# A third attention half turned by the matrix engine ahead of the first MoE unit, and weights of groups two and three brought in one tile a unit

## The chip, the cores and the metric

The kernel runs on one core of a Trainium2 chip. The metric is the device time of one execution in microseconds. Of the engines, TensorE (PE) does the matmuls, VectorE (DVE), ScalarE (ACT) and GpSimd (POOL) the element-wise work, and SyncE (SP) issues nearly all DMA transfers.

## The reference

Three layers follow each other: a linear attention with a gate, a feed-forward layer (called MoE in the code) with a rational activation, and a second one with a softmax-like activation and a layer norm.

```python
# attention: B=4, H=8, S=768, D=48
for t in range(S):
    state = alpha[:, :, t, :, None] * state + np.einsum('bhd,bhe->bhde', k[:, :, t], v[:, :, t])
    y[:, :, t] = np.einsum('bhd,bhde->bhe', q[:, :, t], state)
# layer 1: 3072 tokens x 384 -> 2048 -> 384
h = x @ w_in
P = a[0] + a[1] * h + a[2] * h**2 + a[3] * h**3
Q = 1.0 + np.abs(b[0]) * np.abs(h) + np.abs(b[1]) * h**2
x = (P / (Q + 1e-06)) @ w_out
# layer 2: 384 -> 1024 -> 384
h = x @ w_in2
solu = h * softmax(h)
y = (layernorm(solu) * g_ln) @ w_out2
```

Both layers' weights are 64-bit floats in memory; the attention's inputs are 32-bit.

## The kernel before, in words

**Chunks and halves.** The 768 positions are cut in six chunks of 128 positions by 4 batches, 512 tokens each. A chunk's attention is done in two halves (two batches each), so there are twelve halves, numbered from 0. For a half, keys and queries are needed transposed (head dimension on partitions) and multiplied by running products of the gate alpha. Halves below NPE (two of them, 0 and 1) are turned by TensorE: `a_turn` makes, for each of two parts, three turns (alpha, key, query) of eight matmuls against the identity into a PSUM tile `tp`, on which VectorE runs its scans (`Pp`, `Rp`) and a product; `a_back` turns the keys back on TensorE (`kp`). The other halves are turned by VectorE in `a_dve`: stream transposes, two long scans, a product, two back-transposes, and then a round trip through DRAM (`a_move_qk`, `a_move`) that brings the pieces to their places. The turned query and key then go through `a_pe` on TensorE: scores `sc`, outputs `y`, the state update `u`, and `Sbd`, the state. The result of a half is the layer's input `xt`, in a high and a low part.

**Units.** Layer 1 is cut into 96 units, 16 a chunk, of 128 hidden features. `m_up(u)` does nine 512-column matmuls into `hp`, which lies in one of three PSUM banks with the tag "h". ScalarE makes Abs, two Squares, Ln and Exp of it. VectorE closes the activation with four operations, the last being `fin[u]`; in the "mixed" units (even ones below 24) VectorE has three and GpSimd two. Then `gh` (ScalarE) and `gl` (GpSimd) are the high and the low part, and `m_down` of the unit, nine more matmuls, comes four units later (LAG). A bank of `hp` is free for the unit three later when `fin` is done.

**Weights.** A weight tile comes as 64-bit words (`st` or `words`). `split_w` folds them to 32-bit floats in three VectorE operations (a shift, and two that fold), ScalarE copies the high part and GpSimd subtracts it to leave the low part. Layer 1's weights are in four groups, one for four units of a chunk, of seven tiles each: three of w_in (128x512), four of w_out (128x384). Groups 0 and 1 are folded ahead of unit 0; groups 2 and 3 (`w1_slots`) while units 0 to 7 of chunk 0 run, two tiles a unit. The place in which the folds work on is set by `stage["bank"]`: with "at" or "x2" the middle value `fp` is in PSUM, and with an empty string it is `ft` in SBUF.

**Order.** The instructions' order on each engine is the one in which the code makes them, changed by a planner that hoists an instruction where its inputs allow; `later`, `pin` and `issue_after` keep an instruction behind a given one (`fin` of some units before, for example). In each turn of the main loop the code makes a step of the next half's attention, a weight tile, an up-product and a down-product. HOLD sets from which unit a half's preparation may start, PRE how many weight tiles are folded at four places of the prologue, G1 by how many units the folds stay behind. The coefficients of the activation (the tile `co`) are worked out from a and b in 22 operations on VectorE and ScalarE.

Of the kernel before, what the change touches and what calls it, by code (L numbers as in the profile page):

```python
# [7 lines left out]
F32 = mybir.dt.float32  # L8
# [22 lines left out]
def kernel(  # L31
# [31 lines left out]
    NPE = 2  # L63
    HOLD = {2: (4, 2), 3: (13, 2)}
# [46 lines left out]
    def consts():  # L111
# [16 lines left out]
        nc.vector.tensor_scalar(cf, cf, C_MIN, None, ALU.max)
        nc.vector.reciprocal(rc, cf)
        nc.vector.scalar_tensor_tensor(beta, lin, 0.5, rc, ALU.mult, ALU.mult)  # L130
        nc.vector.tensor_tensor(t, beta, beta, ALU.mult)
        nc.vector.tensor_tensor(t, t, cf, ALU.mult)
        nc.vector.tensor_scalar(bad[:, 4 * NCH + 2:], t, BETA * BETA, None, ALU.is_gt)
        nc.vector.tensor_scalar(beta, beta, B_MAX, -B_MAX, ALU.min, ALU.max)
        nc.vector.tensor_tensor(t, beta, beta, ALU.mult)
        nc.vector.tensor_tensor(base, base, rc, ALU.mult)
        nc.vector.tensor_tensor(rest, base, t, ALU.subtract)
        nc.vector.tensor_tensor(a0s, a0s, rc[:, 1:2], ALU.mult)
        nc.vector.tensor_tensor(back, cf[:, 1:2], rc[:, 0:1], ALU.mult)
        nc.vector.tensor_tensor(back, back, sign, ALU.mult)  # L140
# [972 lines left out]
```

## Time and profile before

| what | value |
|---|---|
| median of three runs | 781.0 us (779.27, 781.0, 783.73) |
| the profiled execution | 778.71 us |
| its span, from the first to the last instruction | 776.7 us |
| granted clock of TensorE, mean | 0.970 |
| TensorE matmul busy | 731.5 us, 94% |
| VectorE busy | 628.9 us, 81% |
| ScalarE busy | 540.3 us, 70% |
| GpSimd busy | 362.5 us, 47% |

The difference of 2.0 us between the profiled execution and its span is what lies around the first and the last instruction. Shares are means over a prologue (attention halves 0 to 2 and two weight groups), the long loop of units, and layer 2, so the bound is read by stretch. Granted clock is in parts of the full 2.4 GHz.

### The profile page before, as it was taken

Reading aid. Unit: us, or ns where it says so; the run is one execution under the profiler, and the core shown is the slowest. Engines: PE = TensorE matmul, PEld = TensorE weight load, DVE = VectorE, ACT = ScalarE, POOL = GpSimd, SP = SyncE. Lnnn points to the kernel's source line nnn. Section 1 sums busy time; section 2 is a strip of 40 time slices with the busy share of each in tenths; the row PEclk is TensorE's granted clock in tenths of the full one; section 3 lists DMA queues with packets and bytes.
Section 4 is the critical chain, followed back from the end, with each engine's and each line's share of the span. In section 5 each row is a group of like instructions: output and inputs, shape, how many; then the busy total and the mean of one; then the engine's idle time right before and its main releaser. Section 6 shows DMA issues by size and latency. Waiting matters only on the chain.

```text
span 776.7 us, 13952 instructions
## 1 busy us (share of the span) xinstructions
PE 731.5 (94%) x4988; PEld 608.4 (78%) x4988; DVE 628.9 (81%) x1097; ACT 540.3 (70%) x998; POOL 362.5 (47%) x314
## 2 busy tenths in 40 slices
PE   4865989999999999999999999999999999999996
PEld 4754777878887787778877788888888989988996
DVE  5997999979998989989898876478887698877630
ACT  3446867867977888788878887788965555555541
POOL 4464878666654355434544433342243343452322
PEclk9957999999999999999999999999999999999999
DMA  7999324275737382717544340730025353541653
GB/s 177 289 295 279 61 81 111 89 224 169 186 121 166 114 207 88 184 47 219 124 144 102 124 82 1 281 127 1 1 82 120 101 131 91 129 111 49 140 118 78
DMA packets 87279, 101.75 MB, mean 131 GB/s; under 512 B 34464, under 2 KB 63136, under 8 KB 87200
## 3 DMA queue, kind: packets, MB, share of 16 engines
q1 hardware_dynamic: 87104, 100.67, 48.0%
q8 instruction: 41, 0.67, 0.4%
q14 instruction: 38, 0.31, 0.1%
q10 hardware_dynamic: 96, 0.10, 0.0%
HBM read 60.59 MB, written 27.56 MB: 113 GB/s over the span
## 4 chain that ended last, share of the span: by engine, by line
DVE 18%; PE 18%; ACT 6%; DMA 3%; SPq 3%; issue 2%; POOL 1%; ACTq 0%; DVEq 0%; POOLq 0%
PE x2p L693 6%; PE hp L648 6%; DVE room L807 3%; SPq L817 3%; DVE room L790 2%; ACT jk L792 2%; PE op L831 2%; DVE sm L786 2%; DVE room L805 2%; PE h L767 2%; DMA L<-room 1%; DVE sm L802 1%; DVE sm L803 1%; DVE p L674 1%; DVE sm L804 1%
## 5 line engine op out<-in xcount | busy, mean ns | idle before, releaser
L682 POOL TENSOR_TENSOR gl<-p,gh 128x512 fp32r<-128x512 f32 x96 | 128.4, 1338 | 198.7 <-ACT gh L681 110.6
L648 PE MATMUL hp<-xt,g 128*128 128x512 f32 x432 | 115.3, 410 | 8.4 <-DVE p L672 7.8
L648 PE MATMUL hp<-xt,w 128*128 128x512 f32 x432 | 110.0, 397 | 4.4 <-DVE p L679 4.4
L648 PEld LDWEIGHTS hp<-xt,g 128*128 128x128 f32 x432 | 82.9, 196 | 29.3 <-DVE p L672 8.0
L831 PE MATMUL op<-w2oh,ln 128*128 128x384 f32 x384 | 101.9, 339 | 0.6 <-DVE ln L823 0.6
L693 PE MATMUL x2p<-gh,g 128*128 128x512 f32 x288 | 100.2, 399 | 2.3 <-ACT x2e L701 2.3
L823 POOL TENSOR_TENSOR ln<-L,ln 128x1024 fp32r<-128x1024 f32 x22 | 54.5, 2482 | 100.8 <-ACT ln L822 96.4
L648 PEld LDWEIGHTS hp<-xt,w 128*128 128x128 f32 x432 | 81.1, 190 | 23.6 <-DVE p L679 5.7
L677 DVE SCALAR_TENSOR_TENSOR w<-w,co,hp 128x512 f32<-128x512 f32 x84 | 62.0, 738 | 44.8 <-ACT hp L676 44.1
L693 PE MATMUL x2p<-gh,w 128*128 128x512 f32 x288 | 96.5, 392 | 0.0
L767 PE MATMUL h<-w2ih,x 128*128 128x512 f32 x288 | 90.8, 394 | 0.0
L655 ACT ACTIVATE p<-hp,co 128x512 f32<-128x512 f32 x96 | 65.8, 685 | 11.1 <-POOL gl L682 10.8
L676 ACT ACTIVATE hp<-ah 128x512 f32<-128x512 f32 x84 | 50.1, 596 | 32.9 <-DVE p L674 32.0
L831 PEld LDWEIGHTS op<-w2oh,ln 128*128 128x128 f32 x384 | 70.1, 188 | 2.2 <-DVE ln L823 1.0
L674 DVE SCALAR_TENSOR_TENSOR p<-p,co,hp 128x512 f32<-128x512 f32 x84 | 61.8, 736 | 9.7 <-ACT p L655 9.1
L656 ACT ACTIVATE w<-ah,co 128x512 f32<-128x512 f32 x96 | 69.3, 723 | 0.4
L693 PEld LDWEIGHTS x2p<-gh,g 128*128 128x128 f32 x288 | 54.6, 191 | 17.5 <-ACT x2e L701 5.0
L653 ACT ACTIVATE ah<-hp 128x512 f32<-128x512 f32 x96 | 56.6, 589 | 14.5 <-PE hp L648 11.5
L681 ACT ACTIVATE gh<-p 128x512 fp32r<-128x512 f32 x96 | 59.9, 624 | 7.9 <-DVE p L679 5.1
L831 PE MATMUL op<-w2ol,ln 128*128 128x384 f32 x192 | 65.0, 339 | 0.0
L693 PEld LDWEIGHTS x2p<-gh,w 128*128 128x128 f32 x288 | 54.1, 188 | 11.7
L767 PEld LDWEIGHTS h<-w2ih,x 128*128 128x128 f32 x288 | 53.9, 188 | 11.7
(183 smaller groups left out, 1569.7 us busy)
## 6 DMA issues: line engine op xcount, KB each, us to landing
L<-room SPq DMA_DIRECT2D x96, 128.0 KB, 2.3
qk_d<-qk SPq DMA_DIRECT2D x10, 771.0 KB, 4.1
st<-in_moe_w_out_dram SPq DMA_DIRECT2D x18, 384.0 KB, 5.0
st<-in_moe_w_in_dram SPq DMA_DIRECT2D x12, 512.0 KB, 4.9
qks<-qk_d SPq DMA_DIRECT2D x20, 257.0 KB, 5.0
ra<-in_alpha_dram SPq DMA_DIRECT2D x48, 96.0 KB, 2.3
rk<-in_k_dram SPq DMA_DIRECT2D x48, 96.0 KB, 2.7
rq<-in_q_dram SPq DMA_DIRECT2D x48, 96.0 KB, 2.4
```

The source lines that it names most:

```text
L648: last["PE", u] = nc.tensor.matmul(hp, lhsT=wi[n](w, kt, o), rhs=xts[c][:, kt, xx, :], start=(kt == 0 and w == 0 and xx == 0), stop=(kt == ...
L653: nc.scalar.activation(ah, hp, AF.Abs)
L655: nc.scalar.activation(p, hp, AF.Square, bias=co[:, 7:8])
L656: nc.scalar.activation(w, ah, AF.Square, bias=co[:, 6:7])
L674: nc.vector.scalar_tensor_tensor(p, p, a1, hp, ALU.add, ALU.mult)
L677: nc.vector.scalar_tensor_tensor(w, w, rest, hp, ALU.add, ALU.mult)
L681: last["ACT", u] = nc.scalar.activation(gh, p, AF.Copy)
L682: last["POOL", u] = nc.gpsimd.tensor_tensor(gl, p, gh[:].bitcast(F32), ALU.subtract)
L693: nc.tensor.matmul(x2ps[c][d], lhsT=wo[n](w, o, d), rhs=gg, start=(f == 0 and w == 0 and gg is gh), stop=(f == NF1 - 1 and w == 1),)
L767: nc.tensor.matmul(hp[:, 512 * n:512 * n + 512], lhsT=x2s[c][:, kt, x, CH * b:CH * b + CH], rhs=w2[w][:, kt, 512 * n:512 * n + 512], start ...
L823: (nc.vector if s in FASTS else nc.gpsimd).tensor_tensor(lo, L, hi.bitcast(F32), ALU.subtract)
L831: nc.tensor.matmul(op, lhsT=x[:, 128 * f:128 * f + 128], rhs=w2[w][:, f, :], start=(f == 0 and x is hi and w == "oh"), stop=(f == NF2 - 1 ...
```

## The change

Six things are changed together. NPE is 3, so that half 2 is turned by TensorE, ahead of unit 0 and into the banks "h", and its round trip through DRAM goes. The coefficients are worked out on GpSimd (but for one reciprocal) after half 0's turn. The words of groups 2 and 3 are asked for at units 0 and 3, and folded one tile a unit in units 1 to 15 except 11, no longer two a unit in 0 to 7. Group 2's folds work in PSUM ("at"), as do those of before; group 3's in SBUF, as before. The preparation of half 4, beside half 3's attention, starts with unit 14 instead of 13, and one weight tile fewer is folded at the second place of the prologue. Units 0 and 2 are not mixed any more.

```diff
-    NPE = 2
-    HOLD = {2: (4, 2), 3: (13, 2)}
+    NPE = 3
+    HOLD = {2:(4,2),3:(14,2)}
...
-    PRE = (1, 1, 0, 0)
+    PRE = (1, 0, 0, 0)
...
-    G1 = 99
+    G1 = 2
+    PACE = {u: 1 for u in range(1, 16) if u != 11}
...
-    MIX = lambda u: u < 24 and u % 2 == 0
+    MIX = lambda u: 3 < u < 24 and u % 2 == 0
...
-        nc.vector.tensor_tensor(back, cf[:, 1:2], rc[:, 0:1], ALU.mult)
+        nc.gpsimd.tensor_tensor(back, cf[:, 1:2], rc[:, 0:1], ALU.mult)
...
-                t = (ps_hp if i < 2 else ps_ap).tile([128, B, CH], F32, name="tp", tag="h" if i < 2 else "at")
+                t = (ps_hp if i < NPE else ps_ap).tile([128, B, CH], F32, name="tp", tag="h" if i < NPE else "at")
...
+        words2 = {}
+
+        def w1_fetch(n):
...
+            words2[n] = (order, t, raw)
+
+        def w1_slots(n):
+            if n not in words2:
+                w1_fetch(n)
+            order, t, raw = words2[n]
+            stage["bank"] = "at" if n == 2 and fast else ""
...
-            _run(a_turn(0), a_pe(0), a_turn(1), a_pe(1), pre)
+            _run(a_turn(0), a_pe(0))
+            coefficients()
+            _run(a_turn(1), a_pe(1), pre)
             clear()
             pre = w1_group(1)
             take(pre, NA)
-            _run(a_load(2, ("ra", "rk")))
-            with tc.issue_after(marks[0, 1].ins):
-                _run(a_prep(2))
-            _run(a_move_qk(2))
+            _run(a_load(2))
...
-                    if f % 4 == 0:
-                        _run(prep)
-                        if f:
-                            stage["bank"] = ""
-                        prep = w1_slots(f // 4 + 2) if f < 8 else iter(())
-                    with later(G1):
-                        take(prep, 1)
+                    if f == 0:
+                        w1_fetch(2)
+                        prep = chain(w1_slots(2), w1_slots(3))
+                    if f == 3:
+                        w1_fetch(3)
...
-                    with later(G1):
-                        take(prep, 1)
+                    with later(G1 if u < NF1 - 4 else 1):
+                        take(prep, PACE.get(u, 0))
```

The line numbers of the kernel after are 8 to 17 higher than before (the turn of `a_turn` is L355 before and L363 after; `split_w`'s three folds are L540, L543, L544 before and L548, L551, L552 after; `fin` is L672 in a mixed and L679 in another unit before, L689 and L696 after).

**TensorE ahead of unit 0.** In the order before, behind the last turn of half 1 (`tp<-ident,rq`) come the matmuls that take the high part off half 0's result (`minus`), half 0's and 1's keys turned back, the scores and outputs of half 1, and then the first up-product (`hp`).

```order
L355 MATMUL tp<-ident,rq 64x128 x6
L466 MATMUL y<-xt,minus 128x256 x3
L385 MATMUL kp<-ident,qks 128x96 x8
L483 MATMUL u<-vns,kns 64x48 x16
L413 MATMUL sc<-qk_403 128x128 x8
L413 MATMUL sc<-qk_404 128x128 x8
L437 MATMUL y<-A,vn_202 32x128 x32
L466 MATMUL y<-xt,minus 128x256 x2
L648 MATMUL hp<-xt,g_136 128x512 x3
L466 MATMUL y<-xt,minus 128x256
```

In the order after, in the same place:

```order
L474 MATMUL y<-xt,minus 128x256 x3
L363 MATMUL tp<-ident,ra 64x128 x8
L393 MATMUL kp<-ident,qks 128x96 x8
L363 MATMUL tp<-ident,rk 64x128 x8
L491 MATMUL u<-vns,kns 64x48
L363 MATMUL tp<-ident,rq 64x128 x8
L491 MATMUL u<-vns,kns 64x48 x15
L421 MATMUL sc<-qk_398 128x128 x4
L363 MATMUL tp<-ident,ra 64x128 x8
L421 MATMUL sc<-qk_398 128x128 x4
L421 MATMUL sc<-qk_399 128x128 x4
L363 MATMUL tp<-ident,rk 64x128 x8
L421 MATMUL sc<-qk_399 128x128 x4
```

Behind it the keys, the turns of half 2 (`ra`, `rk`, `rq`, twice, 48 matmuls in all) now stand among the scores of half 1. The up-product, which had its first three matmuls among the attention's last, comes behind them.

**VectorE at unit 0.** In the order before, from unit 0's first operation (`hp<-p,co,hp`, L666) and unit 1's (L674) to unit 0's last (L672); `words` are group 2's tiles, `Sbd` is half 1's state:

```order
L666 SCALAR_TENSOR_TENSOR hp<-p,co,hp 128x512
L674 SCALAR_TENSOR_TENSOR p<-p,co,hp 128x512
L496 TENSOR_TENSOR Sbd<-u,end 48x8x48 x2
L540 TENSOR_SCALAR fp<-words 128x512 x2
L543 SCALAR_TENSOR_TENSOR fp<-words,fp 128x512
L671 SCALAR_TENSOR_TENSOR hp<-hp,co,ah 128x512
L543 SCALAR_TENSOR_TENSOR fp<-words,fp 128x512
L677 SCALAR_TENSOR_TENSOR w<-w,co,hp 128x512
L544 SCALAR_TENSOR_TENSOR ft<-words,fp 128x512
L672 SCALAR_TENSOR_TENSOR p<-w,hp 128x512
```

After, up to unit 0's last operation (the first L696) and unit 1's (the second):

```order
L691 SCALAR_TENSOR_TENSOR p<-p,co,hp 128x512 x2
L504 TENSOR_TENSOR Sbd<-u,end 48x8x48 x2
L694 SCALAR_TENSOR_TENSOR w<-w,co,hp 128x512 x2
L695 SCALAR_TENSOR_TENSOR hp<-w,hp 128x512 x2
L691 SCALAR_TENSOR_TENSOR p<-p,co,hp 128x512
L548 TENSOR_SCALAR fp<-words 128x512
L696 SCALAR_TENSOR_TENSOR p<-p,co,hp 128x512
L548 TENSOR_SCALAR fp<-words 128x512
L696 SCALAR_TENSOR_TENSOR p<-p,co,hp 128x512
```

Ahead of unit 0's last operation there were five operations on words, now there is one; the unit has four of its own instead of three.

**VectorE at group 3's first tiles.** In the order after, from the last operation of unit 11 (L696) to unit 12's first (L683); `ft<-words` with no `fp` are the folds in SBUF:

```order
L696 SCALAR_TENSOR_TENSOR p<-p,co,hp 128x512
L548 TENSOR_SCALAR ft<-words 128x512
L552 SCALAR_TENSOR_TENSOR ft<-words,ft 128x512
L551 SCALAR_TENSOR_TENSOR ft<-words,ft 128x512
L552 SCALAR_TENSOR_TENSOR ft<-words,ft 128x512
L548 TENSOR_SCALAR ft<-words 128x512
L551 SCALAR_TENSOR_TENSOR ft<-words,ft 128x512
L552 SCALAR_TENSOR_TENSOR ft<-words,ft 128x512
L548 TENSOR_SCALAR ft<-words 128x384
L551 SCALAR_TENSOR_TENSOR ft<-words,ft 128x384
L552 SCALAR_TENSOR_TENSOR ft<-words,ft 128x384
L683 SCALAR_TENSOR_TENSOR hp<-p,co,hp 128x512
```

Before, where the first tile of group 3 is folded, between units 4 (its last operation is just ahead) and 6; `alT` and `qk` are half 3's chain:

```order
L540 TENSOR_SCALAR ft<-words 128x512
L666 SCALAR_TENSOR_TENSOR hp<-p,co,hp 128x512
L678 SCALAR_TENSOR_TENSOR hp<-w,hp 128x512
L309 SCALAR_TENSOR_TENSOR alT<-alT,d_112 128x774
L543 SCALAR_TENSOR_TENSOR ft<-words,ft 128x512
L679 SCALAR_TENSOR_TENSOR p<-p,co,hp 128x512
L671 SCALAR_TENSOR_TENSOR hp<-hp,co,ah 128x512
L312 TENSOR_TENSOR qk<-qk,alT 128x2x3x128
L540 TENSOR_SCALAR ft<-words 128x512
L544 SCALAR_TENSOR_TENSOR ft<-words,ft 128x512
L674 SCALAR_TENSOR_TENSOR p<-p,co,hp 128x512
L672 SCALAR_TENSOR_TENSOR p<-w,hp 128x512
```

Before, the seven tiles stand between the last operation of unit 4 and that of unit 11, one or two operations at a time between the units' own. After, the first four stand nearly without a break between the last operations of unit 11 and the first of unit 12, the other three behind that.

## Rows read from the trace of the kernel before

**Rows 1.** Windows: us, busy us (count) by engine, PEclk, DMA share, GB/s
```profile
40.00:60.00 20.00, 15.33 (x107) 12.99 (x108) 19.92 (x34) 8.98 (x19) 12.19 (x10) 0.51 1.00 279
60.00:80.00 20.00, 12.16 (x72) 9.71 (x71) 15.44 (x28) 13.59 (x25) 11.28 (x11) 0.76 0.97 270
80.00:100.00 20.00, 20.00 (x96) 16.09 (x96) 20.00 (x39) 17.72 (x37) 16.75 (x18) 0.97 0.24 65
```

**Rows 2.** TensorE's timeline: start, us, instructions, in brackets the wait ahead
```profile
75.25 4.21 PE L648 MATMUL hp<-xt,g 128*128 128x512 f32 x9 [7.84 <-DVE p L672]
...
109.12 2.23 PE L648 MATMUL hp<-xt,w 128*128 128x512 f32 x9
...
118.42 3.85 PE L648 MATMUL hp<-xt,w 128*128 128x512 f32 x9 [3.98 <-DVE p L679]
```

**Rows 3.** ScalarE's timeline, end of chunk 0
```profile
170.22 0.69 ACT L701 ACTIVATE x2e<-x2p,co 128x512 f32<-128x512 f32 x1 [1.25 <-DMA w2i_d<-st]
```

**Rows 4.** Groups by line and shape, VectorE, 0 to 65.5 us: half 2's chain
```profile
L300 DVE TENSOR_TENSOR_SCAN P<-alT,d 128x774 f32<-128x774 f32 x1 | 2.5, 2544 | 0.0
L309 DVE TENSOR_TENSOR_SCAN alT<-alT,d 128x774 f32<-128x774 f32 x1 | 2.0, 1980 | 0.0
L316 DVE STREAM_TRANSPOSE alT<-qk 128x384 f32<-128x384 f32 x2 | 1.6, 851 | 0.0
L282 DVE STREAM_TRANSPOSE alT<-ra 128x256 f32<-128x256 f32 x2 | 1.2, 598 | 0.0
L312 DVE TENSOR_TENSOR qk<-qk,alT 128x768 f32<-128x768 f32 x1 | 0.9, 944 | 0.0
L287 DVE STREAM_TRANSPOSE alT<-ra 128x128 f32<-128x128 f32 x2 | 0.8, 384 | 0.0
```

**Rows 5.** The same view: scans and products of halves 0 and 1
```profile
L370 DVE TENSOR_TENSOR_SCAN Rp<-tp,Rp,d 128x127 f32<-128x127 f32 x16 | 6.6, 458 | 0.0
L366 DVE TENSOR_TENSOR_SCAN Pp<-tp,d 128x128 f32<-128x128 f32 x16 | 5.4, 403 | 5.0 <-PE tp L355 5.0
L374 DVE TENSOR_TENSOR qks<-tp,Rp 128x512 f32<-128x512 f32 x2 | 1.4, 685 | 0.1
```

**Rows 6.** The same view: coefficients, the longest and the shortest
```profile
L137 DVE TENSOR_TENSOR co<-co 128x2 f32<-128x2 f32 x1 | 0.7, 726 | 0.0
L121 DVE TENSOR_SCALAR co<-ab 128x1 f32<-128x1 f32 x1 | 0.1, 125 | 0.0
```

**Rows 7.** Groups by line and shape, GpSimd, 0 to 65.5 us
```profile
L427 POOL COPY end<-qks 128x8 f32<-128x8 f32 x1 | 0.2, 190 | 0.0
```

**Rows 8.** SyncE's timeline, the last words of group 1
```profile
49.26 0.37 SPq L533 DMA_DIRECT2D st<-in_moe_w_out_dram  x1
```

**Rows 9.** The page's DMA issues: count, KB each, us to landing
```profile
st<-in_moe_w_out_dram SPq DMA_DIRECT2D x18, 384.0 KB, 5.0
```

**Rows 10.** VectorE's timeline, the last fold of group 1
```profile
62.51 0.55 DVE L544 SCALAR_TENSOR_TENSOR ft<-st,fp 128x384 int32<-128x384 int32 x1 [0.22 <-POOL g L560]
```

**Rows 11.** TensorE's timeline: turns, and keys turned back
```profile
11.11 1.07 PE L355 MATMUL tp<-ident,rk 128*64 128x128 f32 x16
19.15 1.98 PE L355 MATMUL tp<-ident,ra 128*64 128x128 f32 x16 [5.00 <-DMA ra<-in_alpha_dram]
33.39 2.02 PE L385 MATMUL kp<-ident,qks 128*128 128x96 f32 x16 [0.64 <-ACT xt L469]
```

**Rows 12.** The page's costliest groups: an operation of an unmixed unit
```profile
L674 DVE SCALAR_TENSOR_TENSOR p<-p,co,hp 128x512 f32<-128x512 f32 x84 | 61.8, 736 | 9.7 <-ACT p L655 9.1
```

**Rows 13.** Groups by line and shape, VectorE, 60 to 165 us: folds
```profile
L544 DVE SCALAR_TENSOR_TENSOR ft<-words,ft 128x512 int32<-128x512 int32 x3 | 5.3, 1772 | 0.0
L543 DVE SCALAR_TENSOR_TENSOR ft<-words,ft 128x512 int32<-128x512 int32 x3 | 2.7, 897 | 0.0
L540 DVE TENSOR_SCALAR ft<-words 128x512 int32<-128x512 int32 x3 | 2.2, 728 | 0.0
L544 DVE SCALAR_TENSOR_TENSOR ft<-words,fp 128x512 int32<-128x512 int32 x3 | 2.0, 678 | 0.0
```

More of the change, by code (lines that the diff above doesn't have):

```diff
@@ L130, in consts @@
[L130 to L137, printed above, removed]
@@ L138, in consts, with coefficients @@
-        nc.vector.tensor_tensor(a0s, a0s, rc[:, 1:2], ALU.mult)
-        nc.vector.tensor_tensor(back, cf[:, 1:2], rc[:, 0:1], ALU.mult)
-        nc.vector.tensor_tensor(back, back, sign, ALU.mult)
+    def coefficients():
+        sb = const.tile([128, 2], F32, name="sb")
+        nc.gpsimd.tensor_scalar(sb, bb, 0.0, 2.0, ALU.is_ge, ALU.mult)
+        nc.gpsimd.tensor_scalar(sb, sb, 1.0, None, ALU.subtract)
+        nc.gpsimd.tensor_tensor(babs, bb, sb, ALU.mult)
+        cf, lin, rc, beta, rest, t, base = (co[:, 2 * x:2 * x + 2] for x in range(7))
+        nc.gpsimd.tensor_copy(cf[:, 0:1], babs[:, 1:2])
+        nc.gpsimd.tensor_copy(lin[:, 0:1], babs[:, 0:1])
+        nc.gpsimd.tensor_scalar(sign, ab[:, 3:4], 0.0, 2.0, ALU.is_ge, ALU.mult)
+        nc.gpsimd.tensor_scalar(sign, sign, 1.0, None, ALU.subtract)
+        nc.gpsimd.tensor_tensor(cf[:, 1:2], ab[:, 3:4], sign, ALU.mult)
+        nc.gpsimd.tensor_tensor(lin[:, 1:2], ab[:, 2:3], sign, ALU.mult)
+        nc.gpsimd.tensor_tensor(base[:, 1:2], ab[:, 1:2], sign, ALU.mult)
+        nc.gpsimd.tensor_tensor(a0s, ab[:, 0:1], sign, ALU.mult)
+        nc.gpsimd.memset(base[:, 0:1], QC)
+        nc.gpsimd.tensor_scalar(bad[:, 4 * NCH:4 * NCH + 2], cf, C_MIN, None, ALU.is_lt)
+        nc.gpsimd.tensor_scalar(cf, cf, C_MIN, None, ALU.max)
+        nc.vector.reciprocal(rc, cf)
+        nc.gpsimd.tensor_scalar(beta, lin, 0.5, None, ALU.mult)
+        nc.gpsimd.tensor_tensor(beta, beta, rc, ALU.mult)
+        nc.gpsimd.tensor_tensor(t, beta, beta, ALU.mult)
+        nc.gpsimd.tensor_tensor(t, t, cf, ALU.mult)
+        nc.gpsimd.tensor_scalar(bad[:, 4 * NCH + 2:], t, BETA * BETA, None, ALU.is_gt)
+        nc.gpsimd.tensor_scalar(beta, beta, B_MAX, -B_MAX, ALU.min, ALU.max)
+        nc.gpsimd.tensor_tensor(t, beta, beta, ALU.mult)
+        nc.gpsimd.tensor_tensor(base, base, rc, ALU.mult)
+        nc.gpsimd.tensor_tensor(rest, base, t, ALU.subtract)
+        nc.gpsimd.tensor_tensor(a0s, a0s, rc[:, 1:2], ALU.mult)
+        nc.gpsimd.tensor_tensor(back, cf[:, 1:2], rc[:, 0:1], ALU.mult)
+        nc.gpsimd.tensor_tensor(back, back, sign, ALU.mult)
@@ L249, in a_load @@
                     t = slot(3, 2 + x, nm)[:, :16 * D + 16]
-                elif i == 0 and nm == "rq":
+                elif i in (0, 2) and nm == "rq":
                     t = slot(3, 5, nm)[:, :16 * D + 16]
@@ L463, in a_pe @@
                 nc.scalar.activation(hi, y2[z], AF.Copy)
-                if i < NPE + 2:
+                if i < 4:
                     for a in range(n):
@@ L899, in pin @@
             if n <= now[0] < NU and fast:
-                for e, u in (("PE", now[0]), ("ACT", now[0] - n), ("POOL", now[0] - n)):
+                for e, u in (("PE", now[0] if ("PE", now[0]) in last else now[0] - 1), ("ACT", now[0] - n), ("POOL", now[0] - n)):
                     stack.enter_context(tc.issue_after(last[e, u].ins))
@@ L944, in network @@
                 if fast and u < NF1:
[L945 to L951 removed]
+                    if f == 0:
[3 more added lines that the diff above has]
+                        w1_fetch(3)
+                if fast and u == NF1:
+                    _run(prep)
                 m_up(u)
                 if fast and u < NF1:
[L954 to L955 removed]
+                    with later(G1 if u < NF1 - 4 else 1):
+                        take(prep, PACE.get(u, 0))
             if u == NU:
```

13 lines of the change are left out of this document (removed).

## The prediction, written before the changed kernel was run

> **What bounds the kernel now.** I read first the table of busy times by stretch. From 80 us on TensorE is busy all the time, 20.00 of 20 us [rows 1], and what is saved ahead of that point reaches the end of the program, one for one, as long as no new gap opens behind it. Ahead of it VectorE is the full engine: 19.92 of 20 us at 40 to 60, with the DMA engines full as well (share 1.00), while TensorE has 4.7 us free at a granted clock of 0.51. At 80 to 100 VectorE is full again (20.00) beside TensorE: there each unit's VectorE work, the words of weight groups two and three and half 3's chain share one queue. At 60 to 80 VectorE has 4.6 us free, since it waits for ScalarE and for words.
>
> Second I read TensorE's timeline for the gaps in the loop [rows 2]. One is 7.84 us long, up to 75.25: the fourth up-product wants the bank of unit 0, whose last VectorE operation ends at about 75.2. The other is 3.98 us, up to 118.42, for the same kind of reason seven units later. Each is followed by nine matmuls at the lower level, 1.2 GHz: 3.85 us after the second gap, where the same nine take 2.23 us at 109.12. So the gap at 118 costs 3.98 + 1.62 = 5.6 us. Chunk 0's result is first read at 170.22, after a wait of 1.25 us put down to a DMA [rows 3]; behind that I expect no difference.
>
> **The change part by part.** The profiled execution took 778.71 us, of which 776.7 are the span; the median of the three runs is 781.0, 2.3 above it. The sum is made against 778.71, and 2.3 is added at the end.
>
> *Half 2 turned by TensorE, and the coefficients: the prologue.* VectorE loses half 2's chain ahead of unit 0 [rows 4]: scans 2.54 and 1.98, two back-transposes 1.6, three pairs of transposes like the 1.2 one (3.6) and three like the 0.8 one (2.4), and the product 0.94; together 13.0. It gains what one turned half costs [rows 5]: half of 6.6 and 5.4 for the scans (6.0), 1.4 for its two products, and some 0.6 for end values and reciprocals: 8.0. Of the coefficients nineteen operations leave: three long ones, the longest 0.73 and the others estimated at 0.55 each, and sixteen short ones, for which I take 0.14 from the shortest shown, 0.125 [rows 6]; that is 1.8 + 2.2 = 4.0. Net on VectorE: −13.0 + 8.0 − 4.0 = −9.0. In the order of the instructions the same shows: unit 0's first VectorE operations now stand where the last words of group 1 end, with no half-2 transpose between.
>
> GpSimd gets some 27 operations of the coefficients. The nearest row is a copy of 128x8 elements at 0.19 us [rows 7], so 5.1 us, spread over a stretch where it is busy 12.19 of 20 [rows 1]. That work is covered; uncovered it would be the whole 5.1, since unit 0's squares need them.
>
> What VectorE gives up is not all gained, since the words must land. The last words of group 1 are issued at 49.26 and such a transfer lands 5.0 us later [rows 8, 9]; three operations on a 128x384 tile, the last one 0.55 us [rows 10], make 1.65, so 55.9 against 63.06 now (62.51 + 0.55): −7.1 is all that the transfers allow. The queue past which loads move is SP's: half 2's third load comes ahead of the last words, one tile of words fewer does; I set these against each other. TensorE has 48 turning matmuls more ahead of unit 0: sixteen took 1.07 us at 11.11 and 1.98 at 19.15 [rows 11], so 3.2 to 5.9 us, and it has 4.7 free. At the slower price 1.2 would stick out, and the turns share the three banks with the first up-products, so that these can no longer begin among the attention matmuls as three of them do before. I take −6.5, between −4 (turns at the low clock, one bank late by an operation of VectorE) and −9 (the transfers land sooner, since the DMA share falls when half 2's two round trips through memory go).
>
> *Half 2's keys and values in the loop.* Eight more pairs of matmuls that turn half 2's keys back stand in the full stretch: sixteen instructions at 2.02 [rows 11]. TensorE is full there, so +2.0; below, 0, if they fall into one of the gaps of [rows 2].
>
> *Units 0 and 2 not mixed, and the pace.* Each of the two units has one VectorE operation more, 0.736 [rows 12], so +1.5. Unit 0 however now has one word operation ahead of its last, where it had five. Four fewer at 0.68 [rows 13] make −2.7 for the gap at 75. The words come back between units 1 and 8 where VectorE is full, so this holds only as far as TensorE has something to do meanwhile: between −1.2 and +1.5; I take −0.5.
>
> *The gap at 118.* Group 2 comes one tile a unit, so units 4 to 7 carry less and this gap can vanish: −5.6. But the seven tiles of group 3, which stood among units 5 to 11, now begin at unit 11, four of them in a row between the last operation of unit 11 and the first of unit 12, and three more, with half 4's chain, between units 12 and 15. They are in SBUF throughout, and their three operations take 0.73 + 0.90 + 1.77 = 3.4 us a 128x512 tile [rows 13]. So the gap can move there. I take 0 for the two together; the ends are −5.6 and +9.
>
> Sum: −6.5 + 2.0 − 0.5 + 0 = −5.0, so 773.7 for an execution like the profiled one, and 776.0 against the median.
>
> The fold of 1.77 us in SBUF is 2.6 times the same fold with its input in PSUM (0.68) [rows 13]. By the Trainium skill (SBUF — State Buffer, Who interferes with whom) a VectorE instruction with two SBUF inputs contends with a GpSimd instruction that reads SBUF, and the pair of ports is locked for the whole instruction; the trace agrees with its 1.77 to 0.68. By that rule the coefficients on GpSimd would speak against this change too: if each of their 5.1 us held up a two-input operation of VectorE, the prologue would gain 5.1 less, and the sum would be +0.1.
>
> **Rivals.**
> A: the gap at 118 vanishes and nothing takes its place. For it: units 4 to 7 carry one tile each instead of two, and VectorE's work up to unit 15 falls. Against: VectorE stays full from 80 to 140. −5.0 − 5.6 = −10.6, so 770.4.
> B: the gain is eaten by VectorE. Units 12 to 15 each carry a tile of 3.4 beside four operations of 0.736 (2.9), 6.3 a unit, where TensorE needs 4.1 (two times nine matmuls: 4.5 by the nine in 2.23 of [rows 2], 3.75 by the 96 in 20.00 of [rows 1], and I take the middle). Four units fall 2.2 each behind, 8.8; the four units by which down-products lag behind up-products give back about half, 4.1 of it. +4.7 on the forecast: 780.7. For it: the full VectorE of [rows 1]. A second way to the same end: GpSimd's 5.1 us of coefficients hold up VectorE's folds for as long, as the slow fold of [rows 13] beside a busy GpSimd lets one fear; −5.0 + 5.1 gives 781.1. I give it 0.06 of B's chance. The rule of the Trainium skill cited above is that mechanism.
> C: slower. Unit 12's up-product needs the third tile of group 3. Three tiles are 10.2 us of VectorE around the last operation of unit 11; TensorE has cleared the down-products of units 8 to 10 by then and has only unit 11's, half of 4.1, to do. It stands for 8.1 us and comes back at the low clock, 1.6 more: +9.7, 785.7. It decides if the third tile is in place more than about 3.5 us after TensorE has come to that product, which would cost more than the gap at 118 did. Against: if VectorE lags by less than now, the tiles begin sooner.
> That half 2 is not ready for TensorE ahead of unit 0 (its loads late) would take the −6.5 away and leave 782.5; I see it as a part of B.
>
> **How the numbers follow.** Forecast (772 to 779) 0.40, A 0.20, B with what is like it 0.22, C 0.18. The range leaves out the far half of C and the far ends of A: 767.5 to 785.0; for the forecast alone 772 to 779. About 0.5% (3.9 us) is what a measurement of this kernel can tell from no change: faster, below 777.1, is A and most of the forecast, less what B's neighbours take: 0.55. Slower, above 784.9, is most of C: 0.15. Same: 0.30.
>
> **What would show it.** Right, if VectorE's last word operation of group 1 ends near 56.5, the gap ahead of the fourth up-product ends some 7 us sooner, and chunk 0's first read is near 165. The part on the keys is right if sixteen such matmuls stand in the loop at 2 us. A shows as no wait above 1 us on TensorE between 80 and 165; C as one long wait of unit 12's up-product for group 3's third tile, with nine matmuls near 3.9 behind it; B as several short waits for VectorE between units 12 and 16. Wrong altogether, if TensorE's first up-product begins no sooner than now since the turns wait at 0.5 of the clock.

## The result: 0.57% slower, and the profile after

The changed kernel takes 784.96 us (median of 20 runs, 781.32 to 792.07) against 782.16 (20 runs, 777.65 to 786.93): a ratio of 1.0057, interval 1.0035 to 1.0080 (the ratio goes by all the runs; the two medians alone give 1.0036). I had forecast 776.0, a ratio of 0.994. The sign is wrong.

The profiled execution of the kernel after took 787.51 us, with a span of 785.8 and a mean clock of 0.974. It lies 2.5 above its median, as that of before lies under its own, so the two profiles are 9.1 us of span apart where the medians are 2.8 apart. A second profile of each (below) gives 5.8 us. What the two pairs share is the reading. Of the 20 executions 14 lie between 781.3 and 786.4 and six between 787.5 and 792.1, and both profiles (787.51 and 790.82) are like the six, so the waits read below may be longer than those of an execution near the median.

First the windows of the kernel after, columns as in [rows 1]; the last one runs from ScalarE's first operation of unit 3 to that of unit 32.

```profile
40.00:60.00 20.00, 17.65 (x215) 15.19 (x212) 16.83 (x36) 9.04 (x19) 11.53 (x13) 0.86 1.08 293
100.00:120.00 20.00, 19.09 (x190) 16.22 (x183) 13.60 (x21) 17.09 (x33) 13.52 (x13) 1.00 0.15 52
140.00:160.00 20.00, 12.98 (x177) 9.96 (x176) 15.92 (x29) 16.54 (x33) 12.06 (x12) 0.87 0.22 41
160.00:180.00 20.00, 15.90 (x63) 11.85 (x62) 19.37 (x33) 12.74 (x24) 14.64 (x13) 0.96 0.42 136
77.70:253.50 175.80, 160.88 (x1245) 126.88 (x1244) 155.50 (x251) 131.15 (x244) 110.03 (x103) 0.98 0.48 124
```

The same stretch of the kernel before, unit 3 to unit 32:

```profile
79.50:245.80 166.30, 160.62 (x1238) 129.49 (x1238) 157.23 (x248) 129.85 (x240) 114.99 (x105) 0.97 0.51 137
```

So unit 3 is 1.8 us sooner, and the stretch to unit 32 is 9.5 longer (175.8 against 166.3). TensorE's busy time is the same (160.9 and 160.6); its idle time is 14.9 instead of 5.7. Behind unit 32 the two differ by 1.4 (532.3 and 530.9). −1.8 + 9.5 + 1.4 = 9.1, the difference of the spans.

VectorE, full at 40 to 60 in [rows 1], now idles 3.2 us there, and 6.4 at 100 to 120. The gap of [rows 2] at 118 is gone. TensorE's idle time lies at 140 to 190 instead, as its timeline shows (start, us, instructions, the wait ahead):

```profile
73.44 2.07 PE L665 MATMUL hp<-xt,g 128*128 128x512 f32 x4 [6.49 <-DVE p L696]
...
158.51 3.77 PE L665 MATMUL hp<-xt,g 128*128 128x512 f32 x9 [6.04 <-DVE p L696]
...
169.98 2.35 PE L665 MATMUL hp<-xt,g 128*128 128x512 f32 x9 [1.58 <-DVE p L696]
...
176.80 2.33 PE L665 MATMUL hp<-xt,g 128*128 128x512 f32 x9 [2.20 <-DVE alT L302]
...
186.32 2.33 PE L665 MATMUL hp<-xt,g 128*128 128x512 f32 x9 [2.67 <-DVE p L689]
```

The first of these rows is the fourth up-product; the other four are the up-products of units 16, 18, 19 and 21. Their waits make 12.5 us, and the nine matmuls at 158.51 pay 1.4 more at the low clock (3.77 against 2.33). The wait at 158 is for unit 13's last VectorE operation. VectorE's timeline shows why that one is late:

```profile
139.02 1.56 DVE L552 SCALAR_TENSOR_TENSOR ft<-words,ft 128x384 int32<-128x384 int32 x1
142.54 0.76 DVE L683 SCALAR_TENSOR_TENSOR hp<-p,co,hp 128x512 f32<-128x512 f32 x1 [1.97 <-ACT p L672]
144.57 0.76 DVE L688 SCALAR_TENSOR_TENSOR hp<-hp,co,ah 128x512 f32<-128x512 f32 x1 [1.27 <-ACT ah L685]
...
148.01 0.68 DVE L691 SCALAR_TENSOR_TENSOR p<-p,co,hp 128x512 f32<-128x512 f32 x1
...
151.28 1.12 DVE L501 TENSOR_TENSOR Sbd<-Sbd,u 48x384 f32<-48x384 f32 x2
152.44 0.70 DVE L551 SCALAR_TENSOR_TENSOR fp<-st,fp 128x512 int32<-128x512 int32 x1
153.16 2.08 DVE L308 TENSOR_TENSOR_SCAN P<-alT,d 128x774 f32<-128x774 f32 x1
155.17 0.72 DVE L694 SCALAR_TENSOR_TENSOR w<-w,co,hp 128x512 f32<-128x512 f32 x1
...
157.72 0.73 DVE L696 SCALAR_TENSOR_TENSOR p<-p,co,hp 128x512 f32<-128x512 f32 x1
```

Behind group 3's fourth tile (139.02) VectorE has nothing but unit 12, which has only begun, and stands 1.97 and 1.27 us. Unit 12 is late by its own weights, as the rows of TensorE, GpSimd and ScalarE show. In the kernel after, TensorE comes to unit 12 at 132.76, GpSimd makes the low part of group 3's third tile from 138.87 to 140.16, and ScalarE's first operation on the unit starts at 141.34:

```profile
132.76 1.55 PE L665 MATMUL hp<-xt,w 128*128 128x512 f32 x6
...
138.87 1.29 POOL L568 TENSOR_TENSOR w<-ft,w 128x512 fp32r<-128x512 f32 x1 [1.29 <-ACT w L563]
...
141.34 0.60 ACT L670 ACTIVATE ah<-hp 128x512 f32<-128x512 f32 x1 [0.20 <-PE hp L665]
```

In the kernel before, the same part is ready at 122.47, well ahead of unit 12's matmuls:

```profile
121.07 1.40 POOL L560 TENSOR_TENSOR w<-ft,w 128x512 fp32r<-128x512 f32 x1
...
130.03 2.21 PE L648 MATMUL hp<-xt,w 128*128 128x512 f32 x9
```

So the tile is there 7.4 us after TensorE has come to the unit, and TensorE fills that time with other matmuls; VectorE cannot. Then it is overrun: unit 13's first operation (L691) is done at 148.7 and its second (L694) starts at 155.17, behind a fold, transposes and the long scan of half 4, the state (L501) and a tile of the second layer (`fp<-st`). From an idle queue to a pile within ten microseconds. The last of the four waits, at 186, is one step removed: ahead of unit 18's last operation VectorE stands for half 5's alpha, which SyncE asked for only at 175.68, behind half 4's late moves.

```profile
182.91 0.66 DVE L290 STREAM_TRANSPOSE alT<-ra 128x256 f32<-128x256 f32 x1 [3.51 <-DMA ra<-in_alpha_dram]
```

Ahead of unit 0, most of the gain that I had counted is not there. VectorE's last fold of group 1 and the wait that holds it up:

```profile
43.09 1.12 DVE L504 TENSOR_TENSOR Sbd<-u,end 48x384 f32<-48x384 f32 x2 [3.54 <-PE u L491]
...
61.89 0.55 DVE L552 SCALAR_TENSOR_TENSOR ft<-st,fp 128x384 int32<-128x384 int32 x1 [0.75 <-POOL g L568]
```

The last fold ends at 62.44, against 63.06 in [rows 10]: 0.6 us, not 6.5. Up to it the two kernels compare so, before and then after, columns as in [rows 1]:

```profile
0.00:63.06 63.06, 45.13 (x469) 38.18 (x470) 53.89 (x134) 24.18 (x54) 30.92 (x45) 0.78 0.92 253
0.00:62.44 62.44, 48.54 (x565) 42.18 (x566) 47.84 (x118) 24.34 (x51) 34.26 (x75) 0.86 0.91 250
```

VectorE is busy for 6.1 us less (53.89 to 47.84) and idle for 5.4 more, and TensorE has 96 instructions more.

One pair of profiles is a thin base here. In five profiles of kernels with the old order ahead of unit 0 (the kernel before twice, and the runs below with the new pace alone, with the later split and with units 0 and 2 unmixed) the last fold ends at 62.7 to 65.3, 64.0 in the mean, and ScalarE's first operation on unit 0 starts at 64.3 to 67.2, 65.4 in the mean. In nine with the new code there (the kernel after twice and seven runs below) it is 61.1 to 64.2, mean 62.9, and 60.4 to 64.0, mean 62.8. So the last fold comes some 1.1 us sooner and unit 0 some 2.6.

What VectorE waits for at 39.6 to 43.1 is TensorE's state update `u`, and TensorE's timeline shows what stands ahead of it:

```profile
32.70 1.98 PE L363 MATMUL tp<-ident,ra 128*64 128x128 f32 x16 [1.80 <-ACT xt L477]
34.60 3.73 PE L393 MATMUL kp<-ident,qks 128*128 128x96 f32 x16
38.26 1.98 PE L363 MATMUL tp<-ident,rk 128*64 128x128 f32 x16
...
115.10 1.03 PE L393 MATMUL kp<-ident,qks 128*128 128x96 f32 x8
117.85 1.03 PE L393 MATMUL kp<-ident,qks 128*128 128x96 f32 x8
```

The first half of the turns runs at the lower level (1.98 for sixteen, where [rows 11] has 1.07), and the keys with them (3.73 for sixteen, 2.02 there); the granted clock is 0.63 in 30 to 44 us. Each row has sixteen where the order has eight: a turn's matmul shows as two instructions, and half 2's 48 as 96. They take 9.15 us, 5.87 for the 48 instructions up to 44 us and 3.28 for the rest, at 1.09 for sixteen. The last two rows are half 2's keys in the loop, 2.06 us in all.

### The profile page after: what moved, and what is told of

Same layout as the page of the kernel before. It is cut to its first block, busy times and chain, and to the rows that moved or that the text cites. A ratio compares the mean times of both kernels' runs of the same rounds, so it can differ in the third digit from the quotient of the medians.

```text
span 785.8 us, 14174 instructions
## 1 busy us (share of the span) xinstructions
PE 735.2 (94%) x5100; PEld 612.1 (78%) x5100; DVE 621.3 (79%) x1083; ACT 541.1 (69%) x998; POOL 357.0 (45%) x340
## 4 chain that ended last, share of the span: by engine, by line
PE 32%; DVE 17%; ACT 8%; issue 3%; DMA 2%; SPq 2%; POOL 1%; ACTq 0%; DVEq 0%; POOLq 0%
PE h L784 8%; PE x2p L710 8%; PE op L848 7%; PE hp L665 7%; DVE p L691 2%; DVE room L824 2%; DVE w L694 1%; DVE hp L695 1%; ACT jk L809 1%; DVE room L807 1%; DMA rq<-in_q_dram 1%; SPq L834 1%; ACT hp L693 1%; DVE sm L803 1%; ACT gh L698 1%
## 5 line engine op out<-in xcount | busy, mean ns | idle before, releaser
L694 DVE SCALAR_TENSOR_TENSOR w<-w,co,hp 128x512 f32<-128x512 f32 x86 | 63.4, 738 | 43.4 <-ACT hp L693 42.4
L691 DVE SCALAR_TENSOR_TENSOR p<-p,co,hp 128x512 f32<-128x512 f32 x86 | 63.1, 734 | 13.8 <-ACT p L672 13.3
L672 ACT ACTIVATE p<-hp,co 128x512 f32<-128x512 f32 x96 | 66.0, 688 | 10.7 <-POOL gl L699 10.5
L673 ACT ACTIVATE w<-ah,co 128x512 f32<-128x512 f32 x96 | 69.5, 725 | 4.3 <-DVE hp L695 4.1
L696 DVE SCALAR_TENSOR_TENSOR p<-p,co,hp 128x512 f32<-128x512 f32 x86 | 63.7, 741 | 1.2
L710 PEld LDWEIGHTS x2p<-gh,w 128*128 128x128 f32 x288 | 53.8, 188 | 11.9
```

The source lines that it names most:

```text
L672: nc.scalar.activation(p, hp, AF.Square, bias=co[:, 7:8])
L673: nc.scalar.activation(w, ah, AF.Square, bias=co[:, 6:7])
L691: nc.vector.scalar_tensor_tensor(p, p, a1, hp, ALU.add, ALU.mult)
L694: nc.vector.scalar_tensor_tensor(w, w, rest, hp, ALU.add, ALU.mult)
L696: fin[u] = nc.vector.scalar_tensor_tensor(p, p, a0, hp, ALU.add, ALU.mult)
L710: nc.tensor.matmul(x2ps[c][d], lhsT=wo[n](w, o, d), rhs=gg, start=(f == 0 and w == 0 and gg is gh), stop=(f == NF1 - 1 and w == 1),)
```

## The experiments

Each ratio is to the kernel before, timed on the same chip, with its 95% interval. "The pace" is how the tiles of groups 2 and 3 are spread over the units.

**The old pace in the changed kernel.**

```diff
-                    with later(G1 if u < NF1 - 4 else 1):
-                        take(prep, PACE.get(u, 0))
+                    with later(G1):
+                        take(prep, 1)
```
(with G1 = 99, and the tiles taken ahead of the up-product too, as before)

> The changed kernel with only the pace of groups two and three put back (two tiles a unit in units 0 to 7, group 3 among units 5 to 10, no place for the folds behind earlier units). Theory P (the pace costs the time: group 3's tiles and half 4's chain pile up on VectorE in units 11 to 16, where TensorE stood 13.8 us in the profiled execution): that pile goes, the gaps of 6.0, 1.6, 2.2 and 2.7 us between 150 and 190 us go, one of 4 us around 118 comes back; 777 to 781 us, the ratio to the kernel before 0.994 to 1.000. Theory T (the turned half costs it: keys turned back in the full stretch, turns at half clock, VectorE waiting for the state update): 784 to 787, as the changed kernel.

781.75 us, ratio 1.0001 (0.9982 to 1.0019). The whole loss goes with the pace, as theory P says. TensorE's longest wait behind unit 12 is 2.27 at 176; the gap at 118 that P wanted back is 1.44, at 121.

**The new pace alone, in the kernel before.** The edit is the reverse, with all else of the change undone.

> The kernel before with only the new pace (groups two and three one tile a unit, their transfers at units 0 and 3, folds two units behind). Theory P: the pile is there without the turned half, 788 to 792 us, ratio 1.008 to 1.013, a wait above 4 us on TensorE between 140 and 190. Theory T: 780 to 783, ratio within 0.3% of 1.

789.94 us, ratio 1.0100 (1.0072 to 1.0128). Theory P; the same wait stands at the same unit, 16:

```profile
157.92 5.78 PE L658 MATMUL hp<-xt,g 128*128 128x512 f32 x18 [6.68 <-DVE p L682]
```

**The turned half alone, in the kernel before.**

```diff
-    NPE = 2
+    NPE = 3
```
(with the loads and the turn of half 2 as in the change)

> The kernel before with only half 2 turned by TensorE. Theory P: the turned half gains nearly nothing, since VectorE's last word fold of group 1 ended 0.6 us sooner with it, and the keys in the loop cost 2.0: 780 to 784 us. Theory T: 785 to 788. My blind forecast's own reading (6.5 gained in the prologue, 2.0 lost): 777.5.

785.24 us, ratio 1.0033 (1.0016 to 1.0051). Neither theory put it there. Alone it does gain ahead of unit 3, and gives it back behind:

```profile
69.63 3.89 PE L658 MATMUL hp<-xt,g 128*128 128x512 f32 x9 [3.09 <-DVE p L682]
...
87.77 4.21 PE L658 MATMUL hp<-xt,g 128*128 128x512 f32 x9 [4.03 <-DVE p L689]
...
179.71 4.21 PE L658 MATMUL hp<-xt,g 128*128 128x512 f32 x9 [3.22 <-DVE alT L295]
```

The fourth up-product starts at 69.63, 5.6 us sooner than in [rows 2], close to my 6.5; unit 0's first ScalarE operation, where that term was counted, is 3.4 sooner (60.94 against 64.33). Then TensorE waits 4.03 at 88, and 3.22 at 180, with the low clock behind each. Ahead of the second wait VectorE had stood for 9.85 us on a fold of the second layer's weights, until ScalarE had copied half 3's result out of PSUM:

```profile
168.56 0.69 DVE L541 TENSOR_SCALAR fp<-st 128x512 int32<-128x512 int32 x1 [9.85 <-ACT xt L470]
```

In this run the keys of half 0 and the turns behind them run at the upper level, and the granted clock in 30 to 44 us is 1.00:

```profile
34.35 2.02 PE L386 MATMUL kp<-ident,qks 128*128 128x96 f32 x16 [0.64 <-ACT xt L470]
36.92 1.09 PE L356 MATMUL tp<-ident,ra 128*64 128x128 f32 x16 [0.55 <-DMA ra<-in_alpha_dram]
```

**Group 3 folded in PSUM.**

```diff
-            stage["bank"] = "at" if n == 2 and fast else ""
+            stage["bank"] = "at" if fast else ""
```

> The changed kernel with group 3's folds worked out in PSUM as group 2's are, in place of SBUF. Theory P: seven tiles fold about 1.3 us faster each in the pile, 9 us of VectorE less between 125 and 170, of which half reaches TensorE: 779 to 782 us. Theory T: within 1.5 us of the changed kernel's 785. A third view (the PSUM banks are shared with half 3's scores, which then wait): 785 to 788.

786.89 us, ratio 1.0053 (1.0033 to 1.0073): no difference from the change. The third view shows in the trace, though not in the time: a fold now waits for a bank that half 3's scores hold. TensorE's wait of 6 us ahead of unit 16 is not in this run; waits of 1.9, 1.7, 1.4 and 3.5 us between 157 and 182 stand in its place. So the place of the folds is not worth anything here, but what the slow folds cost by themselves is not told apart from the new wait.

```profile
140.73 0.56 DVE L548 TENSOR_SCALAR fp<-words 128x384 int32<-128x384 int32 x1 [7.88 <-ACT A L428]
```

**The small edits alone, in the kernel before** (coefficients on GpSimd, units 0 and 2 not mixed, PRE and HOLD).

> The kernel before with only the small edits: coefficients on GpSimd, units 0 and 2 not mixed, one weight tile fewer at the second place of the prologue, half 4's preparation from unit 14; half 2 turned by VectorE and the pace as before. If the parts add up (turned half alone +0.33%, all but the pace 0.0%), this is 0.3% faster than the kernel before: 779 to 781 us, ratio 0.995 to 0.999. If the small edits do nothing by themselves and only help the turned half (by taking the coefficients out of VectorE's way), the ratio is 0.999 to 1.002.

791.13 us, ratio 1.0103 (1.0077 to 1.0129). Both views are wrong: the edits that I had priced at nearly nothing cost, alone, as much as the pace alone (1.0100).

**Turned half and coefficients with the old pace, units 0 and 2 mixed again.**

```diff
-    MIX = lambda u: 3 < u < 24 and u % 2 == 0
+    MIX = lambda u: u < 24 and u % 2 == 0
```

> The changed kernel with the old pace and with units 0 and 2 mixed again: turned half and coefficients on GpSimd together. The fourth up-product starts 3 to 4 us sooner than in the changed kernel (near 69.5 instead of 73.4, as it did with the turned half alone), since unit 0 has three VectorE operations. If a gain ahead of unit 3 reaches the end, 778 to 780 us, ratio 0.994 to 0.998; if VectorE's full queue behind it takes it back, 781 to 784, ratio 0.998 to 1.003.

786.27 us, ratio 1.0043 (1.0021 to 1.0065), slower than the same kernel with the units unmixed (1.0001). The fourth up-product does start sooner, at 71.40, though not at 69.5; the gain is taken back by waits of 3.15 at 90, 3.39 at 143 (half 3's scores wait for a transfer) and 3.22 at 180. Half 3's result, for which VectorE again stands (7.95 us, up to 169), comes some 4.5 us later than with the units unmixed.

**The kernel before and the kernel after, profiled again**, unchanged.

> A second profile of the kernel before: the spread of single executions, and where in the program it lies. The first profile, 778.7, lies 3.5 below the median of its runs; if chance runs through the whole program, stretches differ by some tenths; if it lies in chunk 0, where VectorE and the transfers decide, the time from unit 3 to unit 32 is some 3 us longer here.

> A second profile of the changed kernel, whose first, 787.5, lies 2.5 above the median of its runs. The waits of TensorE between 140 and 190 us should come again at the same units (16, 17 and on), with 10 to 14 us in all; if the first profile was unlucky in these, less.

The kernel before: 785.29 us, 783.3 of span. Unit 3 is 2.0 us later than in the first profile (the words of group 2 land later), the stretch from unit 3 to unit 32 is the same (166.2 against 166.3), and the rest of the 6.6 comes behind unit 32 (535.6 against 530.9), 3.9 of it behind the last unit's start. So chance lies ahead of unit 3 and behind unit 32, and neither guess was right. The kernel after: 790.82 us, 789.1 of span; unit 3 at 76.2 instead of 77.7; the waits at 157, 169, 175 and 185 are 6.07, 1.00, 2.21 and 2.71, 12.0 in all against 12.5. The pile is the program's, not chance.

**Two tiles a unit in units 1 to 7, all else of the change kept.**

```diff
-    PACE = {u: 1 for u in range(1, 16) if u != 11}
+    PACE = {u: 2 for u in range(1, 8)}
```

> The changed kernel with two tiles a unit in units 1 to 7 in place of one a unit in 1 to 15; all else of the change, the folds' place behind earlier units and the early transfers too, stays. Theory P, sharper: what costs is that group 3's folds stand behind unit 11, since two units behind is not kept and seven of them meet half 4's chain. Here group 3 is folded between units 5 and 11 by the order, so the waits between 150 and 190 us shrink to under 5 us in all: 779 to 783 us, ratio 0.996 to 1.001, as with the old pace. If the place behind earlier units or the early transfers cost it, the ratio stays at 1.005 or more.

782.63 us, ratio 1.0002 (0.9975 to 1.0030). One edit to the table takes the whole loss away; the early transfers and the rule that keeps the folds behind earlier units are innocent. TensorE's wait for a bank at 158 is gone, and the only one above 1 us behind unit 11 is 1.59 at 164.65. It waits 2.13 and 2.56 at 102 and 106 instead, for banks that folds hold, so its idle time from unit 3 to unit 32 is 9.7 us, between 14.9 of the change and 5.7 before.

**The second layer's weights split from unit 23 on**, with the old pace, and in the kernel before.

```diff
-    U2, IDLE = NF1 - 1, (0, NF1 // 2 - 1)
+    U2, IDLE = NF1 + 7, (0, NF1 // 2 - 1)
```

> The kernel with the old pace, and the second layer's weights split from unit 23 on instead of 15. With the old pace VectorE stood 4.8 us at 165 us on the first operation of such a tile, which wants a PSUM bank that half 3's attention still holds, with units 15 and 16 queued behind it. If that block is what takes back the gain ahead, 776 to 780 us, ratio 0.992 to 0.997. If it only moves to the next half, ratio 0.998 to 1.002.

> The kernel before with the same later split. The kernel before shows no wait of VectorE above 1.1 us there, so nothing should change: ratio 0.998 to 1.002, 781 to 784 us. A gain of 0.3% or more would say that the later split helps by itself.

782.32 us, ratio 1.0006 (0.9990 to 1.0022), and 784.40, ratio 1.0017 (0.9999 to 1.0036). In the first the wait on that tile is gone, and VectorE stands 5.48 us at 165 for half 3's state instead: the block only moved. The second is a change that cannot be told from none.

**Half 4's preparation from unit 13, with the old pace.**

```diff
-    HOLD = {2:(4,2),3:(14,2)}
+    HOLD = {2:(4,2),3:(13,2)}
```

> The kernel with the old pace, and half 4's preparation from unit 13, as before the change, instead of 14. If the single unit matters little, within 0.2% of the old pace's 1.0001, 780.5 to 784 us. If the chain of half 4 one unit sooner runs ahead of unit 16's and takes the wait at 176 us away (2.3 and 1.6 for the low clock), 778 to 780.

781.43 us, ratio 0.9989 (0.9969 to 1.0010). No difference, and the wait is still there (3.23 at 178). It has the lowest ratio of all, but it does not beat the kernel before.

**Half 4's preparation from unit 16, in the changed kernel.** The same line with 16.

> The changed kernel with half 4's preparation from unit 16 instead of 14: group 3's tiles stay behind unit 11, but half 4's transposes and scans no longer stand among them. If the chain is what makes unit 13's last operation late, the wait of 6.0 us ahead of unit 16's up-product goes below 2: 780 to 783 us, ratio 0.998 to 1.002. If the seven tiles alone do it, the wait stays above 4 and the ratio at 1.004 or more; and half 4, then late itself, can cost as much at unit 20 and behind.

784.12 us, ratio 1.0028 (1.0005 to 1.0050). Between the two readings: with half 4's chain out of the way, the wait ahead of unit 16's up-product is half as long.

```profile
154.85 3.86 PE L665 MATMUL hp<-xt,g 128*128 128x512 f32 x9 [3.10 <-DVE p L696]
```

By this one pair of profiles the late tiles make one half of that wait and their meeting with half 4 the other. In the whole time the two kernels are not told apart with certainty, since 1.0028 and 1.0057 have overlapping intervals.

**The changed kernel with half 2 turned by VectorE.** The reverse of the edit on NPE.

> The changed kernel with half 2 turned by VectorE as before; pace, coefficients, unmixed units stay. The pace alone gave 1.010 and the small edits alone 1.010; if both costs stand, 1.012 to 1.020 (791 to 798 us), and the turned half is worth 0.6 to 1.4% here. If the two costs are one and the same (VectorE late in units 0 to 16), 1.008 to 1.011.

789.33 us, ratio 1.0089 (1.0069 to 1.0110): the costs of the pace and of the small edits are not added but shared. Within the rest of the change the turned half seems worth 0.3% (the intervals of 1.0089 and 1.0057 overlap a little); alone it costs 0.3%.

**Units 0 and 2 unmixed, and nothing else, in the kernel before.**

> The kernel before with units 0 and 2 unmixed and nothing else. If that edit is the costly one of the small ones, 1.007 to 1.011 (787 to 791 us), with the gap ahead of the fourth up-product above 10 us, where it was 7.8 and 11.4 in two profiles of the kernel before. By my forecast's own price for it (two operations more, 1.5 us, less what unit 0 gains), 0.998 to 1.002.

787.29 us, ratio 1.0066 (1.0041 to 1.0091). This edit carries most of the small edits' cost (1.0103, with an interval that overlaps this one); the coefficients, PRE and HOLD were not moved alone. My price for it was wrong. The gap ahead of the fourth up-product is 12.45 us:

```profile
81.90 4.21 PE L648 MATMUL hp<-xt,g 128*128 128x512 f32 x9 [12.45 <-DVE p L679]
```

Part of that gap is chance, since VectorE first waits for the words of group 2, 1.38 and 3.45 us in the two profiles of the kernel before and 2.88 here. First the row of the kernel before, then that of this run:

```profile
69.95 1.29 DVE L540 TENSOR_SCALAR fp<-words 128x512 int32<-128x512 int32 x2 [1.38 <-DMA words<-in_moe_w_in_dram]
...
73.50 1.29 DVE L540 TENSOR_SCALAR fp<-words 128x512 int32<-128x512 int32 x2 [2.88 <-DMA words<-in_moe_w_in_dram]
```

From that first fold to the fourth up-product it is 5.3 us in both profiles of the kernel before (75.25 − 69.95, 77.21 − 71.91) and 8.4 here (81.90 − 73.50). So 3.1 us are the order's.

## Why the prediction was wrong

**The prologue (−6.5).** This step failed in the changed kernel: 1.1 us came at the last fold and 2.6 at unit 0, by the means above. Three of its parts were wrong.

The matmuls were counted by half. I priced 48 turning matmuls by rows that count instructions, sixteen in 1.07 or 1.98, and each of these matmuls is two instructions. By my own rows the 96 cost 6.4 to 11.9 us, not 3.2 to 5.9, so the 4.7 us that TensorE had free could not cover them. They took 9.15.

VectorE's −9.0 was added up from single operations' durations. By these the measured loss up to the last fold is 8.6, but in the trace the operations overlap, and of the engine's time it is 6.1.

The wait was not seen. Of the 6.1 us 5.4 turn into idle time, 3.54 of them in the wait for the state update, in the order of VectorE's queue. At the low clock the keys of half 0 that share the stretch grow as well, by 1.7 (3.73 against 2.02), and `u` stands behind all of it. I had the doubled price in the bounds, but as something that sticks out at the end of TensorE's work, not as a wait of VectorE ahead of its folds. My sign of being wrong altogether came too: TensorE's first up-product begins at 55.36, against 54.11 before.

The turned half alone, with the coefficients still on VectorE, had no such wait. That the coefficients on GpSimd undo the gain by letting VectorE come to the state sooner is argued from the order, and from waits for it of 1.7 to 3.9 us in the runs that have both edits and none above 1 us with the turned half alone. It is not shown: no run moved them alone, and that run's one profile, with unit 0 at 60.9, is no sooner than the soonest of those with both edits, 60.4.

**Units 0 and 2 unmixed (−0.5).** Wrong in sign at unit 0. I counted the five word operations that leave unit 0's chain and not what comes in. The order after shows it: L694, L695 and L691 come in pairs, so unit 1's and unit 2's operations now stand ahead of unit 0's last one. With the old pace, from unit 0's first ScalarE operation to the fourth up-product it takes 10.8 (74.12 − 63.35), and 7.8 with units 0 and 2 mixed again (71.40 − 63.58): 3.0 lost, close to the 3.1 of the run that has this edit alone. In the kernel before it cost 0.66% of the whole, some 5 us.

**The keys in the loop (+2.0).** Right: 2.06 in the rows at 115 and 118.

**The gap at 118 (0).** This is the step that set the sign. The gap vanished, as rival A said (−5.6), and more came back at 140 to 190: idle time from unit 3 to unit 32 is 9.2 us longer in the first pair of profiles and 8.4 in the second (14.2 against 5.8). Against a term of 0 that is the miss. I had put the two ends at −5.6 and +9 and taken a value between them, though nothing in the rows held the two in balance: the order already showed four tiles in a row behind unit 11. The measured value lies at the upper end. The premise of the whole sum, that what is saved ahead of 80 us reaches the end as long as no new gap opens, was not tested by it, since the gaps opened.

**The rivals.** What came has C's cause, B's place and C's price. C's condition held: the third tile of group 3 was in place 7.4 us after TensorE had come to unit 12, and C asked for 3.5. But TensorE did not stand there, as C said; it had scores, down-products and the first matmuls of units 13 and 14 to do. The lateness went to VectorE, which ran dry behind the tiles (1.97 and 1.27 us) and then had units 12 to 14 and half 4's chain at once; so TensorE waited later, for VectorE's last operation of units 13 and on, which is B. B's sum went by the four units' extra work, 8.8 less half, and left both out. The run with half 4's chain later took half of the main wait away. That C's 785.7 lies close to the measured 785.0 is in part luck: its 8.1 us of standing and 1.6 of low clock were for another wait than the 6.04 and 1.4 that came at unit 16, and the rest is made up of three more waits.

B's second way, GpSimd's coefficients holding up the folds, did not come: the folds ahead of unit 0 take 0.55, as in [rows 10]. Those have one input in PSUM, and in both traces such folds take 0.51 to 0.69 with GpSimd at work beside them or not. Of group 3's folds in SBUF the Trainium skill (SBUF — State Buffer, Who interferes with whom) lets one expect what the rows at the end show, 1.25 and 1.33 us. The run in PSUM took these slow folds away and put a wait of 7.88 in their place, so what they cost in the pile was not measured.

**Profile and medians.** I added 2.3 to go from the profiled execution to the median. The medians of before are now 782.2 to 783.0, so 3.5 to 4.3 would have been right; this is 1.2 to 2 us of a miss of 9.

**What stays open.** With the pace undone the change is worth nothing (1.0001, 1.0002), and its parts don't add up: the small edits cost 1.03% alone, the turned half 0.33% alone, both together 0.0%. The coefficients on GpSimd, PRE and HOLD were moved only with other edits. Each part leaves VectorE, half 3 and the units of chunk 0 in another order, and a gain ahead turned into waits for half 3's result near 165 to 180 in four runs. Why the unmixed units cost 0.66% in one setting and save 0.4% in the other was not settled: the traces show the 3 us lost ahead of unit 3 in both, and half 3's result some 4.5 us sooner with them in the second, but not what sets that result.

## What to carry to other kernels

When work on a shared queue is spread out, ask what it meets where it is put, and read the order there: here one tile a unit left VectorE idle for 6.4 us at 100 to 120, brought the weights of unit 12 too late, and piled up VectorE's queue at 147 to 170; with two tiles a unit the loss was gone. Before pricing a row, check that it counts what the order counts. A saving ahead of the bottleneck counts only if nothing on the saved engine's queue waits for the engine that took the work over, at the clock that this engine has there. Where two large terms of opposite sign stand in one line of a sum, their middle is no forecast.

## What the runs showed that I had not expected

The same sixteen key turns took 2.02 us in the kernel before and with the turned half alone, and 3.73 in the kernel after, where the granted clock was 0.63 in 30 to 44 us, behind waits of TensorE of 1.17 and 1.80. What brought the clock down there is not shown: the turned half alone has the same turns behind the keys and a clock of 1.00.

Folds in SBUF shared their delay differently from one kernel to the other: 0.90 and 1.77 in [rows 13], and in the kernel after, by groups of line and shape at 60 to 180 us,

```profile
L552 DVE SCALAR_TENSOR_TENSOR ft<-words,ft 128x512 int32<-128x512 int32 x3 | 4.0, 1328 | 0.1
L551 DVE SCALAR_TENSOR_TENSOR ft<-words,ft 128x512 int32<-128x512 int32 x3 | 3.8, 1250 | 0.0
```

nearly the same sum (2.58 against 2.67). The delay goes with GpSimd's work beside the fold. Of the 28 folds of this kind at 60 to 180 us in the two traces (the second and third operation of a tile, both inputs in SBUF), six have no GpSimd operation beside them and take 0.51 to 0.66 us, as with an input in PSUM; the 19 that have GpSimd beside them for 0.5 us or more take 0.70 to 1.88. Two of the kernel before, the first with GpSimd idle, the second with GpSimd busy throughout:

```profile
110.74 0.66 DVE L543 SCALAR_TENSOR_TENSOR ft<-words,ft 128x512 int32<-128x512 int32 x1
...
113.50 1.88 DVE L544 SCALAR_TENSOR_TENSOR ft<-words,ft 128x512 int32<-128x512 int32 x1
```

And single executions of one kernel differ by 6.6 us of span while 166.3 us of it, from unit 3 to unit 32, repeat within 0.1 in the kernel before; in the kernel after the same stretch took 175.8 and 177.7.
